# A gated linear attention and a squared-ReLU network on one core: scores as 64-by-64 tiles, a new order at the front, and another queue for the last store

## The chip, the core and the metric

The kernel runs on one core of a Trainium2 chip. A core has five engines with instruction streams of their own: TensorE (PE in the profile; PEld is its weight load), VectorE (DVE), ScalarE (ACT), GpSimd (POOL) and SyncE (SP), which here only issues transfers. ScalarE and GpSimd issue transfers too. The metric is the device time of one execution in microseconds, as the median of several runs.

## The reference

For each of 4 sequences and 8 heads of width 48 the attention runs a complex state over 768 tokens, and the tokens it gives go through a feed-forward network with 2048 hidden values:

```python
mag = np.sqrt(a_re * a_re + a_im * a_im)
scale = np.minimum(mag, 0.999) / (mag + 1e-06)
ar, ai = a_re * scale, a_im * scale
for t in range(S):                        # per batch and head, D = 48
    S_re, S_im = ar * S_re - ai * S_im + k[t] v[t]^T, ar * S_im + ai * S_re
    y[t] = q[t] @ S_re
x = y as (batch * S, heads * 48)          # 3072 x 384
h = np.maximum(x @ w_in, 0.0)             # w_in 384 x 2048
out = (h * h) @ w_out                     # w_out 2048 x 384
```

The two weight matrices arrive as 64-bit floats, that is as pairs of 32-bit words; the kernel turns them into 32-bit floats on the chip ("decoding").

## The kernel before

**Work and tiles.** A chunk is 128 tokens of one sequence. Two sequences go side by side, so that 12 groups of two chunks are worked one after the other: in the plan below the chunk of the first sequence of group g is called a*g*, the other b*g*. Eight heads lie on the 128 partitions in pairs: head rows 0 to 47 and 64 to 111, and the last pair's heads in the gaps of 16 rows between them ("gap" transfers fill these from the input; "last heads" copies bring their products into place again, L901).

For a chunk, `make_operands` turns raw gates, queries and keys into scaled operands on VectorE and ScalarE: squares (L773), sum of squares (L787), two steps of an inverse root (L792 to L805), gates (L825 to L829), running products in blocks and over blocks, and four products `qk` (L895). After the fourth product SyncE copies the last heads (`last<-qk`, L901). Then `chunk` does the attention: `scores` first applies the state carried from the chunk before (y, L936; not for the first chunk of a sequence) and then builds the scores of the chunk (a_ps, L944); keys are turned (tp, L951), the scores masked on VectorE (L963), summed over values (y, L970), the tokens copied to x (L981), and the new state added up (add, L994). The feed-forward network follows: `first_product` (h_ps, L1047 for single chunks in the first two groups, L1063 for both chunks later), squared ReLU on ScalarE, and the second product (o_ps, L1083 and L1153).

**The order of the work** is written out by hand: `FRONT` (L1187) is a string of some 1,400 tokens, and `follow` calls one function for each in that order, which fixes the order on every engine's stream and on every queue. The letters that matter here: `M` small preparations (`turn_mask`: M0 warms a function table on ScalarE, M1 builds the mask, M2 to M8 are memsets on VectorE), `l` loads of features (`load_parts`, L505), `v` loads of values, `f` and `j` fetch a weight block's words on SyncE and GpSimd, `D` and `A` are the two VectorE steps of decoding a block (L632 the shift, L635 the low part, with `U` and `S` on ScalarE ahead of the latter), `p`, `q` and `o` steps of `make_operands` for an a chunk, a b chunk or both, `a` and `b` steps of `chunk`, `g` gap copies of x, `F` and `H` first product and squared ReLU, `T`, `Z`, `R` parts of the second product and its sums, `s` stores, `K` a last test of ranges.

**Scores.** For each of four pairs, two components and two head rows one matmul has a stationary operand of 48 rows and 128 columns and 128 moving columns: 16 matmuls, which the profile shows as 32 rows. The two head rows lie in different halves of the array's rows. y L936 does its work with stationary operands of 48 by 64.

**Loads of features** (L519, L529): for each chunk and half of the rows one large transfer, followed on its queue by small gap transfers; SyncE takes one half, ScalarE or GpSimd the other.

**Stores** (L1117): all on SyncE, but for the last chunk, whose left half is stored by ScalarE and right half by SyncE. Behind them each engine loads a count (L1362) and jumps over a second way of computing (L1363), which is not taken; a closing barrier ends the program.

Of the kernel before, what the change touches and what calls it, by code (L numbers as in the profile page):

```python
# [32 lines left out]
ROWS = 64  # L33
LEVELS = 7
HALF = 64
RE, IM = 0, 1
# [390 lines left out]
def quotient_path(ctx, tc, feat, vtok, w_in, w_out, w1, w2, out, n_seq, count):  # L427
# [77 lines left out]
    def load_parts(gi, part=None, second=False, only=None):  # L505


        part = None if part == 2 else part
        parts = [slice(A_RE, Q), slice(Q, V), slice(A_RE, V)][2 if part is None else part]
        queues = [nc.sync, nc.scalar if part == 0 else other if gi < TWO_QUEUES else nc.sync]  # L510
        if part != 0 and gi < TWO_QUEUES:
            queues[not second] = None
        for b, n in enumerate(groups[gi]):
            if only not in (None, b):
                continue
            for hh, queue in enumerate(queues):
                if queue is None:
                    continue
                queue.dma_start(  # L519
                    out=raw[rows(hh), parts, b].rearrange("d x g t -> d x (g t)"),  # L520
                    in_=feat[n, hh, :, parts, 0:NG].rearrange("d x g t -> d x (g t)"))

                if part == 0 and b:
                    queue = nc.gpsimd
                gap = raw[pads(hh), parts, b]
                rest = feat[n, hh].rearrange("(r g) x p t -> r x g p t", g=NG)[:, parts, :, NG]
                for i in range(min(gap.shape[1:3])):
                    at = (slice(None), i) if gap.shape[1] < NG else (slice(None), slice(None), i)
                    queue.dma_start(out=gap[at], in_=rest[at])  # L529

    def in_turn(rows_, n):

# [382 lines left out]
    def chunk(gi, b):  # L915
# [7 lines left out]
        def scores():  # L923
# [17 lines left out]
            for p_ in range(NP):  # L941
                for c in (RE, IM):
                    for hh in range(HH):
                        nc.tensor.matmul(ps[:, hh, p_], lhsT=operand(2 + c, p_, rows(hh)),  # L944
                                         rhs=operand(c, p_, rows(hh)), start=(c == RE),
                                         stop=(c == IM))

        def keys_turned(c):
            tp = tiles["tp"] = pm.tile([C, NG, P], F32, tag="m", name="tp")
# [161 lines left out]
    def store(i, b):  # L1111

        queue, cols = nc.sync, slice(0, DM)
        if i == NGR - 1 and b:
            queue, cols = (nc.scalar, slice(0, MH)) if b == 1 else (nc.sync, slice(MH, DM))
        b = min(b, 1)
        queue.dma_start(out=in_turn(out, groups[i][b])[:, :, cols], in_=out_of[i, b][:, cols])  # L1117

# [38 lines left out]
    def outputs(i, r):  # L1157
# [27 lines left out]


    FRONT = (  # L1187
        "M8 l0.0.0 M2 M3 M7 l0.0.1 M1 M0 p0.0 p0.1 p0.3 p0.4 p0.5 p0.7 p0.2 q0.0 q0.3 p0.8 p0.9 "
        "p0.10 q0.4 q0.5 p0.11 q0.7 l0.1.0 f0 f1 l0.1.1 v0.0 f2 i0.1.0 j0 j2 q0.1 p0.12 p0.22 "
        "q0.8 q0.2 U0 q0.9 p0.6 q0.10 S0 p0.15 p0.23 p0.24 D0 p0.25 M4 p0.13 M5 p0.16 q0.11 "  # L1190
        "p0.26 i0.1.1 j1 D1 p0.27 A0 p0.17 p0.14 j3 i1.2.0 U1 S1 U2 q0.12 p0.18 q0.6 S2 q0.22 "
        "A1 f4 l1.2.0 f3 j4 p0.19 q0.15 p0.20 q0.23 p0.28 q0.24 p0.29 q0.25 p0.30 q0.16 D2 "
        "q0.26 q0.13 q0.27 A2 q0.17 p0.21 f6 a0.1 a0.2 U3 q0.14 a0.0 a0.3 U4 S3 q0.18 p1.6 a0.4 "
        "S4 a0.5 a0.6 l1.2.1 a0.7 D3 q0.19 M6 a0.8 q0.28 q0.20 p1.0 p1.3 q0.29 D4 q0.30 i1.2.1 "
        "q1.0 p1.4 p1.5 j6 j5 p1.1 p1.2 j7 g0.0 f5 v0.1 q0.21 f7 p1.7 p1.10 p1.9 p1.8 A3 A4 "
        "F0.1.0 U5 a0.9 U6 S5 D5 b0.1 b0.0 p1.11 b0.2 p1.12 S6 H0.1.0 A5 U7 b0.3 b0.4 S7 p1.15 "
        "D6 p1.23 b0.5 F0.0.0 b0.6 b0.7 f8 p1.24 A6 p1.25 q1.3 p1.16 D7 p1.26 A7 p1.27 D8 p1.17 "
        "F0.2.0 H0.0.0 q1.4 H0.2.0 U8 p1.22 S8 F0.3.0 b0.8 H0.3.0 p1.18 p1.13 p1.14 A8 g0.1 f11 "
        "F0.2.1 f9 f10 v1 p1.19 p1.20 p1.28 D9 p1.29 p1.30 q1.5 U9 q1.1 H0.2.1 q1.7 D11 b0.9 "
        "D10 F0.3.1 T0.0.0 H0.3.1 S9 A9 U10 q1.8 S10 q1.9 q1.2 q1.10 F0.0.1 F0.1.1 p1.21 f12 "  # L1200
        "f13 A10 q1.6 U11 q1.11 q1.12 S11 U12 a1.0 a1.1 T0.1.0 a1.5 a1.6 a1.7 S12 D13 D12 A11 "
        "q1.15 q1.23 A12 T0.2.0 T0.3.0 a1.2 U13 H0.0.1 q1.22 H0.1.1 a1.3 T0.4.0 q1.24 q1.25 "
        "q1.16 q1.26 q1.13 q1.27 q1.17 f14 g1.0 f15 S13 q1.14 l2 F1.2.0 H1.2.0 A13 F1.0.0 "
        "F1.3.0 q1.18 a1.4 U14 H1.3.0 U15 S14 i2 S15 q1.19 q1.28 q1.20 q1.29 D14 q1.30 A14 D15 "
        "A15 q1.21 a1.8 T0.5.0 F1.1.0 T0.6.0 T0.7.0 o2.0 o2.1 o2.3 o2.4 E0.0 o2.5 o2.2 b1.0 "
        "o2.7 a1.9 b1.5 T0.0.1 T0.1.1 b1.3 T0.2.1 b1.6 T0.3.1 T0.4.1 T0.5.1 T0.6.1 T0.7.1 o2.8 "
        "o2.9 o2.10 H1.1.0 b1.7 s0.0 v2 g1.1 w0 o2.11 o2.12 o2.15 o2.22 o2.13 o2.6 H1.0.0 "
        "F1.0.1 F1.1.1 E0.1 o2.14 b1.4 H1.1.1 l3 T1.0.0 b1.1 H1.0.1 F1.3.1 T1.1.0 T1.2.0 T1.3.0 "
        "T1.4.0 T1.5.0 T1.6.0 T1.7.0 o2.23 o2.24 o2.25 o2.16 o2.26 o2.27 o2.17 o2.18 o2.19 "
        "o2.28 o2.20 o2.29 o2.30 F1.2.1 o3.0 o3.6 o3.3 o3.4 o3.5 b1.2 o3.7 E1.0 b1.8 b1.9 o2.21 "  # L1210
        "a2.0 a2.5 t0 a2.1 T1.0.1 T1.1.1 o3.2 o3.1 o3.8 a2.2 o3.10 o3.9 a2.3 a2.6 a2.4 a2.7 "
        "H1.2.1 o3.11 o3.12 W0 a2.8 b2.0 a2.9 o3.22 H1.3.1 b2.5 T1.2.1 T1.3.1 b2.6 T1.4.1 "
        "T1.5.1 T1.6.1 b2.7 T1.7.1 g2 F2.0 o3.13 o3.15 o3.23 o3.24 o3.25 o3.16 o3.26 o3.27 "
        "o3.17 o3.14 H2.0 o3.18 o3.19 o3.28 o3.20 o3.29 o3.30 F2.2 H2.2 F2.4 H2.4 l4 s1.0 b2.1 "
        "F2.1 o4.0 H2.1 o3.21 s0.1 v3 F2.6 H2.6 b2.2 o4.3 F2.5 F2.7 o4.2 o4.4 o4.5 H2.7 X2.0 t1 "
        "X2.2 Y2.2 t3 H2.5 Y2.0 o4.7 b2.3 a3.0 b2.4 E1.1 s1.1 X2.1 Y2.1 a3.5 Z2.1 b2.8 a3.6 "
        "o4.1 o4.8 o4.9 Q2.0 b2.9 a3.3 a3.7 o4.10 a3.4 o4.11 F2.3 H2.3 Z2.0 a3.1 b3.0 X2.3 R2.0 "
        "o4.6 o4.22 Z2.3 a3.2 b3.5 b3.6 b3.7 o4.12 Y2.3 o4.13 Q2.3 Q2.1 o4.15 o4.23 Q2.2 o4.24 "
        "a3.8 a3.9 Z2.2 R2.3 Z2.5 o4.14 R2.2 R2.5 R2.1 o4.25 o4.16 o4.26 o4.27 o4.17 g3 F3.2 "
        "H3.2 F3.0 b3.3 b3.4 Z2.4 H3.0 o4.18 o4.19 o4.20 o4.28 o4.29 o4.30 F3.4 H3.4 F3.6 R2.4 "  # L1220
        "H3.6 X3.2 X3.0 F3.5 F3.1 b3.1 H3.5 F3.7 w1 l5 o5.0 t2 Z2.6 o5.3 o5.1 o5.4 H3.1 b3.2 "
        "o5.5 R2.6 o5.7 X3.1 o4.21 s2.1 s2.0 W1 w2 v4 F3.3 H3.3 H3.7 o5.2 Z3.0 b3.8 a4.0 X3.3 "
        "b3.9 Y3.1 Y3.2 a4.1 a4.5 Y3.0 Z3.1 R3.0 o5.6 o5.9 a4.2 o5.8 a4.3 Q3.0 o5.10 R3.1 o5.11 "
        "Q3.2 Y3.3 a4.6 a4.4 a4.7 a4.8 b4.0 a4.9 b4.1 Z3.2 Z3.3 o5.12 o5.22 b4.2 W2 b4.3 b4.4 "
        "R3.2 b4.5 b4.6 R3.3 b4.7 b4.8 o5.15 o5.23 o5.24 o5.25 Q3.1 Q3.3 o5.16 o5.13 Z3.4 Z3.5 "
        "w3 g4 o5.14 R3.4 o5.26 R3.5 F4.5 H4.5 l6 o5.27 o5.17 o5.18 o5.19 o5.20 v5 o5.28 F4.1 "
        "H4.1 X4.1 o5.29 F4.0 F4.4 o5.30 H4.0 o6.0 W3 H4.4 o6.3 b4.9 F4.3 Z3.6 H4.3 o6.4 F4.2 "
        "H4.2 o6.5 R3.6 o6.2 o6.1 F4.6 o6.7 H4.6 o5.21 s3.0 a5.0 F4.7 s3.1 o6.9 o6.8 a5.5 a5.6 "
        "o6.10 a5.7 H4.7 Z4.0 b5.0 Z4.1 Y4.1 o6.11 X4.3 Y4.3 X4.0 o6.6 w7 o6.22 o6.12 W7 R4.0 "
        "b5.5 X4.2 o6.15 Y4.0 Q4.0 R4.1 b5.6 Y4.2 Q4.1 Z4.2 R4.2 b5.7 o6.23 o6.24 Q4.2 o6.25 "  # L1230
        "o6.16 Z4.3 o6.13 Q4.3 o6.26 Z4.4 R4.3 Z4.5 R4.5 o6.27 o6.17 R4.4 o6.14 g5 F5.2 H5.2 "
        "o6.18 F5.4 F5.0 H5.4 o6.19 o6.28 o6.20 o6.29 o6.30 F5.3 Z4.6 l7 w6 H5.0 W6 a6.3 F5.1 "
        "o7.1 R4.6 H5.3 H5.1 F5.6 o7.0 H5.6 a6.4 X5.0 o7.3 o7.4 o7.5 F5.7 s4.0 o6.21 w8 v6 F5.5 "
        "a6.0 v7 a6.1 Z5.0 H5.5 W8 H5.7 o7.2 a6.2 w4 s4.1 X5.2 a6.5 Y5.0 Y5.2 o7.7 a6.6 a6.8 W4 "
        "o7.9 o7.8 R5.0 o7.10 b6.0 w9 W9 a6.7 Z5.1 X5.1 a6.9 b6.5 Q5.0 X5.3 Q5.2 Y5.1 Y5.3 R5.1 "
        "o7.11 Z5.2 o7.12 b6.3 R5.2 b6.4 Z5.3 b6.1 Z5.4 Q5.3 o7.15 o7.23 o7.24 o7.25 Q5.1 o7.16 "
        "w5 R5.3 b6.2 o7.22 W5 R5.4 b6.6 b6.8 Z5.5 Z5.6 b6.7 w10 g6 F6.1 o7.13 o7.26 o7.27 R5.5 "
        "o7.14 o7.6 o7.17 o7.18 o7.19 o7.28 o7.20 o7.29 o7.30 H6.1 F6.6 F6.5 l8 R5.6 H6.6 W10 "
        "v8 o7.21 s5.0 w14 s5.1 H6.5 F6.2 H6.2 F6.0 o8.0 o8.2 H6.0 b6.9 X6.2 Y6.2 o8.3 F6.4 "
        "a7.1 F6.3 o8.4 o8.5 H6.3 o8.6 H6.4 a7.0 a7.5 X6.1 a7.2 F6.7 H6.7 o8.1 X6.0 o8.7 o8.8 "  # L1240
        "o8.10 Z6.0 a7.3 R6.0 o8.9 Z6.1 Y6.0 X6.3 Y6.3 Y6.1 Q6.0 Q6.2 Z6.2 a7.4 W14 a7.6 a7.7 "
        "R6.2 a7.8 o8.11 a7.9 b7.0 Q6.3 R6.1 b7.5 w13 W13 o8.12 b7.1 b7.2 o8.22 Z6.3 R6.3 o8.13 "
        "o8.15 Q6.1 o8.23 o8.24 b7.6 b7.3 Z6.4 b7.7 b7.4 g7 o8.14 Z6.5 o8.25 R6.5 o8.16 o8.26 "
        "o8.27 o8.17 R6.4 b7.8 F7.5 F7.0 H7.5 o8.18 H7.0 F7.1 w15 W15 H7.1 l9 F7.4 o8.19 o8.28 "
        "o8.20 o9.0 H7.4 F7.2 F7.6 H7.2 o8.29 X7.1 o8.30 o9.3 o9.4 o9.5 o9.7 Y7.1 o9.1 Z6.6 "
# [150 lines left out]
```

## Time and profile before

| | us |
|---|---|
| median of 3 runs | 664.95 (664.70 to 665.57) |
| the profiled execution | 666.06 |
| its span, first to last instruction | 664.1 |
| PE busy | 616.7 |
| DVE busy | 493.2 |
| ACT busy | 434.9 |
| mean granted clock of PE | 0.996 |

The span is cut into 40 slices of 16.6 us; a digit is the busy share of a slice in tenths. The chain of waits is followed back from the last instruction, at each step to what released it. In a table of groups "xcount" counts rows, and one matmul of 32-bit floats makes two rows. Some rows of this profile that are used later (busy us and mean ns of one row; then idle time of the engine ahead of them):

| group | rows | busy, mean | 
|---|---|---|
| L944 a_ps<-qk, 48x128 by 128 | 576 | 39.9, 287 |
| L944 a_ps<-last, 48x128 by 128 | 192 | 15.8, 280 |
| L936 y, 48x64 by 128 | 640 | 22.8 + 12.2, about 275 |
| L994 add, 128x64 by 48 | 640 | 23.0, 226 |
| L1047 h_ps, 128x128 by 128 | 384 | 46.4, 281 |

A mean here is the length of a row in the pipeline, and rows overlap; the pace is read from the chain.

### The profile page before, as it was taken

Reading aid. Unit: us, or ns where it says so; the run is one execution under the profiler, and the core shown is the slowest. Engines: PE = TensorE matmul, PEld = TensorE weight load, DVE = VectorE, ACT = ScalarE, POOL = GpSimd, SP = SyncE. Lnnn points to the kernel's source line nnn. Section 1 sums busy time; section 2 is a strip of 40 time slices with the busy share of each in tenths; the row PEclk is TensorE's granted clock in tenths of the full one; section 3 lists DMA queues with packets and bytes.
Section 4 is the critical chain, followed back from the end, with each engine's and each line's share of the span. In section 5 each row is a group of like instructions: output and inputs, shape, how many; then the busy total and the mean of one; then the engine's idle time right before and its main releaser. Section 6 shows DMA issues by size and latency. Waiting matters only on the chain.

```text
span 664.1 us, 13108 instructions
## 1 busy us (share of the span) xinstructions
PE 616.7 (93%) x5147; PEld 552.0 (83%) x5147; DVE 493.2 (74%) x981; ACT 434.9 (65%) x847; POOL 31.9 (5%) x74
## 2 busy tenths in 40 slices
PE   0068999999999999999999999999999999999996
PEld 0057987776889899989899899899999899989996
DVE  4999888979997969858849948968849858753030
ACT  7668989757584585494586785686685675644331
POOL 5230110000000000000000000000000000000000
PEclk9998999999999999999999999999999999999999
DMA  8986863540634331730842813542631620232101
GB/s 198 167 160 148 257 192 68 92 56 21 95 72 82 55 87 32 119 73 10 142 142 55 142 51 79 96 109 72 113 95 32 108 65 21 67 84 79 47 26 30
DMA packets 41744, 60.41 MB, mean 91 GB/s; under 512 B 5832, under 2 KB 29896, under 8 KB 41672
## 3 DMA queue, kind: packets, MB, share of 16 engines
q1 hardware_dynamic: 39360, 55.39, 38.7%
q0 software_dynamic: 1824, 3.64, 3.0%
q8 instruction: 42, 0.69, 0.5%
q10 hardware_dynamic: 488, 0.44, 0.2%
q14 instruction: 30, 0.25, 0.1%
HBM read 48.76 MB, written 4.72 MB: 81 GB/s over the span
## 4 chain that ended last, share of the span: by engine, by line
PE 91%; DVE 5%; DMA 2%; ACT 1%; issue 1%; ACTq 0%; POOL 0%; DVEq 0%; SPq 0%
PE h_ps L1063 31%; PE o_ps L1153 28%; PE a_ps L944 7%; PE o_ps L1083 6%; PE h_ps L1047 6%; PE y L970 4%; PE y L936 3%; PE add L994 3%; PE tp L951 2%; DVE ab L494 1%; DMA last<-qk 1%; DVE pr L494 1%; DMA raw<-in_feat_dram 1%; DVE qk L494 0%; DMA words<-in_moe_w_in_dram 0%
## 5 line engine op out<-in xcount | busy, mean ns | idle before, releaser
L1063 PE MATMUL h_ps<-x,w 128*128 128x256 f32 x960 | 212.4, 379 | 0.0
L1063 PEld LDWEIGHTS h_ps<-x,w 128*128 128x128 f32 x960 | 180.9, 190 | 24.1 <-ACT h L1070 0.2
L1153 PE MATMUL o_ps<-w,h 128*128 128x192 f32 x640 | 110.5, 328 | 0.0
L1153 PEld LDWEIGHTS o_ps<-w,h 128*128 128x128 f32 x640 | 103.8, 190 | 1.9 <-issue 0.5
L1070 ACT ACTIVATE h<-h_ps 128x512 f32<-128x512 f32 x80 | 47.5, 594 | 69.5 <-PE h_ps L1063 67.3
L494 DVE TENSOR_TENSOR pr<-ab 128x384 f32<-128x384 f32 (+3 forms) x196 | 70.1, 375 | 4.3 <-ACT ab L833 0.9
L1153 PE MATMUL o_ps<-w_sum,mix 128*128 128x192 f32 x320 | 55.3, 328 | 0.0
L494 DVE TENSOR_TENSOR a<-a_ps,mask 128x1024 f32<-128x1024 f32 x24 | 29.3, 1222 | 33.6 <-PE a_ps L944 33.5
L494 DVE TENSOR_TENSOR ab<-pr 128x48 f32<-128x48 f32 (+3 forms) x210 | 49.9, 260 | 5.3
L1153 PEld LDWEIGHTS o_ps<-w_sum,mix 128*128 128x128 f32 x320 | 51.7, 190 | 0.7 <-issue 0.2
L1071 ACT ACTIVATE h<-h 128x512 f32<-128x512 f32 x80 | 50.5, 631 | 2.5
L951 PE MATMUL tp<-ident,qk 128*128 128x128 f32 x120 | 21.5, 291 | 30.3 <-DVE qk L494 30.0
L1047 PEld LDWEIGHTS h_ps<-x,w 128*128 128x128 f32 x384 | 45.6, 197 | 4.0 <-DVE w L494 1.3
L1047 PE MATMUL h_ps<-x,w 128*128 128x128 f32 x384 | 46.4, 281 | 2.2 <-DMA x<-x 1.1
L494 DVE TENSOR_TENSOR qk<-ab,qk 128x768 f32<-128x768 f32 (+1 forms) x56 | 46.1, 842 | 1.0
L1083 PE MATMUL o_ps<-w,h 128*128 128x384 f32 x128 | 44.3, 492 | 0.0
L951 PEld LDWEIGHTS tp<-ident,qk 128*128 128x128 f32 x120 | 14.8, 146 | 35.3 <-issue 31.7
L981 ACT COPY x<-y 64x256 f32<-64x256 f32 (+1 forms) x72 | 26.5, 368 | 24.9 <-PE y L970 23.4
L944 PE MATMUL a_ps<-qk 48*128 48x128 f32 x576 | 39.9, 287 | 0.0
L494 DVE TENSOR_TENSOR mix<-h 128x256 f32<-128x256 f32 x40 | 16.8, 420 | 30.9 <-ACT h L1071 30.9
L758 ACT ACTIVATE qk<-raw 128x768 f32<-128x768 f32 (+1 forms) x28 | 37.4, 1341 | 3.6 <-DVE raw L494 3.6
L494 DVE TENSOR_TENSOR room<-ab,carry 128x1344 f32<-128x1344 f32 (+1 forms) x28 | 36.8, 1354 | 3.6 <-ACT carry L874 2.8
(106 smaller groups left out, 923.4 us busy)
## 6 DMA issues: line engine op xcount, KB each, us to landing
raw<-in_feat_dram SPq DMA_DIRECT2D x40, 288.0 KB
words<-in_moe_w_out_dram SPq DMA_DIRECT2D x8, 768.0 KB
again<-in_moe_w_in_dram SPq DMA_DIRECT2D x16, 384.0 KB
again<-in_moe_w_out_dram SPq DMA_DIRECT2D x16, 384.0 KB
last<-qk SPq DMA_DIRECT2D x48, 97.5 KB
words<-in_moe_w_in_dram SPq DMA_DIRECT2D x8, 576.0 KB
vt<-in_vtok_dram SPq DMA_DIRECT2D x24, 192.0 KB
out_dram<-o SPq DMA_DIRECT2D x23, 192.0 KB
```

What stands on the lines that cost most here:

```text
L494: nc.vector.tensor_tensor(out=out, in0=in0, in1=in1, op=op)
L758: nc.scalar.activation(out=out.rearrange("p c j n -> p c n j"), func=AF.Copy, in_=in_.rearrange("p c (n j) -> p c n j", j=L), **kwargs)
L944: nc.tensor.matmul(ps[:, hh, p_], lhsT=operand(2 + c, p_, rows(hh)), rhs=operand(c, p_, rows(hh)), start=(c == RE), stop=(c == IM))
L951: nc.tensor.transpose(tp[:, g], qk_of[gi % 2][:, b, g, 2 + c, 0:C], ident)
L970: nc.tensor.matmul(tiles["y"][p_ % 2][crossed(hh, p_), p_ // 2], lhsT=v[:, columns(hh, at)], rhs=tiles["am"][:, hh, p_], start=(first and ...
L981: nc.scalar.copy(out=x_of[gi][to, odd::2, b * C:(b + 1) * C], in_=tiles["y"][odd][of, 0:NP // 2])
L1047: nc.tensor.matmul(ps[:, j], lhsT=w1_blocks[:, k, g, at:at + P], rhs=x_of[i][:, g, b * C:(b + 1) * C], start=(g == 0), stop=(g == NG - 1))
L1063: nc.tensor.matmul(ps[:, j], lhsT=w1_blocks[:, k, g, at:at + P], rhs=x_of[i][:, g], start=(g == 0), stop=(g == NG - 1))
L1070: nc.scalar.activation(out=h, in_=h_ps[i, f], func=AF.Relu, scale=of_w1)
L1071: nc.scalar.activation(out=h, in_=h, func=AF.Square)
L1083: nc.tensor.matmul(o_of[i, b], lhsT=tokens_of(i, f, b)[:, j], rhs=w2[:, k], start=(k == 0), stop=(k == NFB - 1))
L1153: nc.tensor.matmul(to, lhsT=x(k)[:, j], rhs=factor(z)[:, 2 * k + j], start=(z in (0, 1, 3) and k == j == 0), stop=(k == KH // 2 - 1 and j ...
```

## The change

In `load_parts` the gap transfers of the first part (gates) of a chunk a0 go ahead of the large one on their queue; for the other parts the order stays:

```diff
-                queue.dma_start(
-                    out=raw[rows(hh), parts, b].rearrange("d x g t -> d x (g t)"),
-                    in_=feat[n, hh, :, parts, 0:NG].rearrange("d x g t -> d x (g t)"))
-
-                if part == 0 and b:
-                    queue = nc.gpsimd
                 gap = raw[pads(hh), parts, b]
                 rest = feat[n, hh].rearrange("(r g) x p t -> r x g p t", g=NG)[:, parts, :, NG]
-                for i in range(min(gap.shape[1:3])):
-                    at = (slice(None), i) if gap.shape[1] < NG else (slice(None), slice(None), i)
-                    queue.dma_start(out=gap[at], in_=rest[at])
+                pieces = [(slice(None), i) if gap.shape[1] < NG else (slice(None), slice(None), i)
+                          for i in range(min(gap.shape[1:3]))]
+                moves = [(gap[at], rest[at]) for at in pieces]
+                whole = (raw[rows(hh), parts, b].rearrange("d x g t -> d x (g t)"),
+                         feat[n, hh, :, parts, 0:NG].rearrange("d x g t -> d x (g t)"))
+                if part == 0 and b:
+                    queue.dma_start(out=whole[0], in_=whole[1])
+                    queue = nc.gpsimd
+                else:
+                    moves.insert(len(moves) if part == 0 else 0, whole)
+                for to, of in moves:
+                    queue.dma_start(out=to, in_=of)
```

In `scores` each matmul becomes two, one for each half of the stationary columns and of the output's partitions:

```diff
-                        nc.tensor.matmul(ps[:, hh, p_], lhsT=operand(2 + c, p_, rows(hh)),
-                                         rhs=operand(c, p_, rows(hh)), start=(c == RE),
-                                         stop=(c == IM))
+                        for s in (slice(0, ROWS), slice(ROWS, C)):
+                            nc.tensor.matmul(ps[s, hh, p_],
+                                             lhsT=operand(2 + c, p_, rows(hh))[:, s],
+                                             rhs=operand(c, p_, rows(hh)), start=(c == RE),
+                                             stop=(c == IM), skip_group_check=True)
```

Both halves of the last chunk's store are issued by SyncE:

```diff
-            queue, cols = (nc.scalar, slice(0, MH)) if b == 1 else (nc.sync, slice(MH, DM))
+            cols = slice(0, MH) if b == 1 else slice(MH, DM)
```

The plan has the same tokens in another order up to F4.1, the first product of group 4; from there on it is unchanged. Its beginning, and the part around the last heads of chunk b0 (q0.21):

```diff
-        "M8 l0.0.0 M2 M3 M7 l0.0.1 M1 M0 p0.0 p0.1 p0.3 p0.4 p0.5 p0.7 p0.2 q0.0 q0.3 p0.8 p0.9 "
...
-        "q1.0 p1.4 p1.5 j6 j5 p1.1 p1.2 j7 g0.0 f5 v0.1 q0.21 f7 p1.7 p1.10 p1.9 p1.8 A3 A4 "
...
+        "l0.0.0 l0.0.1 M1 M0 p0.0 p0.1 p0.3 p0.4 p0.5 p0.7 M2 M3 p0.2 q0.0 q0.3 M8 M6 M7 p0.9 "
...
+        "D5 q0.29 q1.3 q0.30 U5 p1.4 p1.5 g0.0 f6 F0.1.0 S5 q0.21 p1.7 A4 a0.9 b0.1 p1.2 p1.10 "
+        "p1.8 p1.9 p1.1 U6 b0.2 p1.11 A5 b0.0 f7 v0.1 p1.12 H0.1.0 S6 U7 p1.22 p1.15 b0.5 p1.23 "
```

Numbers of lines shift by 3 to 5 in the changed kernel.

## The prediction

> **What bounds the kernel now.** I read the page's slices first, then the chain of waits for the whole span, then that chain in windows, then groups by shape. The slices say which stretch belongs to whom:
>
> ```profile
> PE   0068999999999999999999999999999999999996
> DVE  4999888979997969858849948968849858753030
> PE 91%; DVE 5%; DMA 2%; ACT 1%; issue 1%; ACTq 0%; POOL 0%; DVEq 0%; SPq 0%
> ```
>
> The reader is to see two regimes. In the first three and a half slices (to about 58 us) TensorE (PE) is mostly idle and VectorE (DVE) full; from there to the last slice PE is full, and the chain gives it 91% of the span. A change counts for what it takes off PE's work after 58 us, for what it does to the moment at which PE becomes continuous, or for the last 6 us. The table of stretches has PE busy 20.00 of 20 us in 60 to 80 us, 200.00 of 200 in 300 to 500: after 58 us there is no idle time to win, only work.
>
> The window of the chain at 185 us shows what a scores block costs in place:
>
> ```profile
> 185.58 1.03 PE y L936 x32
> 186.61 1.99 PE a_ps L944 x32
> 188.60 2.80 PE o_ps L1153 x16
> 191.39 1.07 PE add L994 x32
> 196.42 2.60 PE o_ps L1153 x16
> 206.19 0.92 PE add L994 x32
> ```
>
> (start, length, engine, tile, line, rows; a matmul is two rows in this trace.) The same 16 rows of o_ps take 2.60 us behind other 128-by-128 work and 2.80 behind a scores block; add takes 1.07 behind o_ps and 0.92 behind y L970 of its own shape. So each change of tile shape on PE costs 0.15 to 0.20 us.
>
> The last view is the chain at the front, where PE waits:
>
> ```profile
> 49.92 0.08 SPq L901
> 50.05 6.70 DMA last<-qk
> 56.79 0.71 PE a_ps L944 x6
> 58.25 3.81 PE h_ps L1047 x22
> ```
>
> The copy of the last heads of chunk b0 leaves SyncE (SP) when VectorE has made the fourth product, takes 6.70 us, and the last scores of that chunk wait for it; PE is continuous from there.
>
> **The change part by part.**
>
> *Scores as 64 by 64.* Each of 24 blocks goes from 32 rows (48x128 stationary, 128 moving columns) to 64 rows (48x64). Streaming: 12 rows of h_ps L1047 with 128 columns take 1.34 us, 0.111 a row, over the whole array. 16 pairs of 64x128 tiles are 16 x 0.111 = 1.78; the block takes 1.99, so 0.21 is the price of entering its shape. y L936 already has 64x64 tiles: 32 rows as 8 fours are 0.89 of its 1.03, entry 0.14. The new block is 16 fours, again 1.78. What goes is the entry, where y L936 stands right ahead in the same shape: 20 blocks (all but the first chunk of each of the four sequences). 20 x 0.19 (between 0.14 and 0.21) = 3.8; the four others swap an entry of 0.21 for 0.14, 0.3. Sum -4.1 us, all on PE's path.
>
> Here a rule speaks against the change. The Trainium skill, "TensorEngine Tiling (Array Packing)", section Instruction Overhead, gives each matmul some 60 cycles that don't shrink, and warns against taking a tiling factor from what is already small. At the 2.4 GHz of "Trainium Kernel Development and Optimization", NeuronCore Architecture, that is an estimated 25 ns; put on top of the 32 added rows of each block it is 768 x 25 ns = 19 us lost, not 4 won. The rows say otherwise: y L936 runs 32 rows of just this shape in 1.03 us with its entry, add L994 32 rows of 48 columns in 0.92 (28.7 ns a row). As a floor of 28.7 against 27.8 from streaming, it costs 64 x 0.9 ns x 24 = 1.4 us. I take y's pace, the same shape, and keep -2.7 as the end of the range. The same page, Key Properties, says that a change of tiling mode drains PE: that is the entry seen above.
>
> *The plan's order on PE.* Counting shape changes along both plans, with the scores already fused, gives 101 before and 98 after (y L970 and add stand together more often): 3 x 0.17 = -0.5. From F4.1 (about 320 us) the plans are equal.
>
> *The front on ScalarE and the transfers.* "Table warmed first": in the changed program ScalarE's order is still DMA issues, table load, the two mask copies, table load, warm-up, squares. In the profile the loads are 1.28 us each, at 3.27 and 5.93, and the first squares start at 7.33. Nothing is removed: 0. The gap transfers ahead of the large one concern only chunk a0 of the first part; SP and ScalarE issue as many as before (0.6 to 0.8 us each). The large transfers of chunk a0 leave 1.4 to 1.7 us later, at about 2.6; transfers issued at that time landed in 3 to 3.7 us, so at 6.3 at most, under cover of the table load to 7.2. Without that cover it would be 0.6 to 1 us. I take 0 (0 to +0.5).
>
> *The front on VectorE.* The memsets M8, M2, M3, M7 lay in its idle time before 8.19 (5.05 us waiting for the first squares). They now stand behind the first inverse: begun 0.70, qk 0.15, states 0.78, 1.63 us. VectorE still waits there for ScalarE (1.24, 0.24 and 0.82 us before 9.98, 11.38 and 12.76); the first wait is ahead of them, the two others take up 1.0. So +0.65 at the second inverse. Up to the fourth product of chunk b0 the new order also has one more decode low part (w<-w,part, 0.87), one more shift (L632, 0.50) and one sum of squares of group 1 (L787, 0.48). Walking both orders row by row they are level at 42.4 us (one decode went later), and behind it stand two decodes, a shift and a sum of squares more: 2 x 0.87 + 0.50 + 0.48 - 0.1 (memset kt, gone ahead) = +2.6. The fourth product ends at 52.0 in place of 49.35, and SP's copy, queued behind it, leaves then.
>
> What that costs depends on the copy's own time. Before, a weight fetch (47.44) and the value load vt (47.96) went out just ahead of it, the next fetch just behind at 50.74: 6.70 us. The same copy for chunk a0 at 35.46, with nothing near, was done when GpSimd took it at 39.05: 3.6 us. Afterwards vt is moved behind it, past the next fetch, and the fetch ahead leaves about 4 us earlier than it. So landing is 55.6 at 3.6, 58.7 at 6.7; I take 56.0, near the free one: -0.7. The moved vt, behind the fetch on the queue, should land by 59; its reader y L970 of chunk b0 also needs the mask product, which VectorE reaches at about 60.0 (58.54 to 59.67 before), behind 24 rows of h_ps. The later decodes of blocks 4 to 7 end at 57 to 65 us, before PE's need. I take no new stall in 58 to 170 us, with +1 for the range.
>
> One more term: at 58.25 these 24 rows took 4.03 us where 2.68 is usual (granted clock 0.65 in 58 to 62.2). PE waits as long as before; I leave that 1.35 as it is, and a gain of it for the range.
>
> *The last store.* ScalarE issues it at 658.50 in 1.20 us, loads the count (0.69) and jumps; its first instruction behind the jump is at 663.17. SP's issues of stores take 0.60 to 0.71, so the data land some 0.5 earlier. But SP is now the late one: its branch comes at about 659.2 in place of 656.63, and SP needed 3.9 us from there to its next instruction (ScalarE 2.6, GpSimd 2.8, VectorE 3.5), then a row of some 20 semaphore waits at 0.065, 1.3, which it did under cover of ScalarE. 659.2 + 2.6 to 3.9 + 1.3 + 0.9 for the closing barrier = 664.0 to 665.3 against 664.1. Middle value +0.4 (-0.1 to +1.2).
>
> **Sum** against the profiled execution (span 664.1, its time 666.06): -4.1 - 0.5 + 0 - 0.7 + 0.4 = -4.9, 661.2. It is 1.1 over the median of the runs; on 664.95 the same sum gives 660.0.
>
> **The rivals.**
> 1. *The front takes some back.* For: VectorE is full there (9.86 of 10 us in 50 to 60), and 2.6 us are put before the copy. Against: the queue is freer. With 6.7 again (+1.9) and the tail's +1.2: -4.6 + 3.1 = -1.5, 663.4. Chance 0.14.
> 2. *The front gives more.* The copy at 3.6 (-1.1) and no lowered clock (-1.35), tail -0.1: -4.6 - 2.5 - 0.1 = -7.2, 657.7. Chance 0.13.
> 3. *Slower: the column halves don't overlap.* Two halves of one row group read the same moving rows; if they run one after the other, a row costs 55 ns, a block 64 x 0.0555 = 3.55 + 0.14, +1.7 x 24 = +41, 706 us. It decides from 31 ns a row (1.99 / 64). Against it: y L936's fours at 27.8. Chance 0.06.
> 4. *The change doesn't do what it says.* For the table this is so already. If the entry stays too, because each block waits for its first weights whatever its shape, -4.1 becomes 0 and the rest cancels: 664.5. Against: add's 0.92 behind its own shape. Chance 0.03.
>
> **How the numbers follow.** The sum above, 660.0, has chance 0.64; with its terms' ends (-2.7 to -4.5 for scores, -0.5 to +1.5 for the front, -0.1 to +1.2 for the tail), not all at one end, 658 to 662.5. The range reaches to rivals 1 and 2: 656.9 to 663.6. A measurement of this kernel tells 0.2%, 1.3 us, from no change. Cases 1 (in the main) and 2 and the likeliest are faster: 0.91; same 0.03; slower 0.06.
>
> **What would show it.** Right: a block of 64 rows of a_ps in 1.78 to 1.85 us behind y L936, with h_ps or o_ps behind it still 0.2 longer; squares again near 7.3; the last<-qk copy of chunk b0 issued near 52 and landed near 56; PE full from about 57; SP the last engine at the end. Wrong: rows of a_ps at over 31 ns; a copy landing at 58 or later; PE idle between 60 and 170 us for a weight or mask; squares waiting for the feature load.

## The result and the profile after

| | before | after |
|---|---|---|
| median of 6 runs each, us | 664.92 (664.63 to 665.57) | 661.35 (659.45 to 661.95) |
| the profiled execution | 666.06 | 661.44 |
| its span | 664.1 | 659.1 |
| time outside the span | 1.96 | 2.34 |
| PE busy | 616.7 | 611.2 |

The medians differ by 3.57 us, 0.54%. The ratio of the runs, which is not the quotient of the medians, is 0.9937 (95% interval 0.9924 to 0.9951); it stands for 4.2 us, between 3.3 and 5.1. Four of the six runs after lie between 661.2 and 662.0 and two near 659.5. The point forecast was 660.0, that is 4.95 us. By the medians 1.35 of them did not come, but 4.95 lies just inside the interval.

First the slices and the shares of the chain of waits in the profile after:

```profile
PE   0059999999999999999999999999999999999995
DVE  4999997998999948968759858879859858743030
PE 77%; DVE 10%; ACT 6%; DMA 5%; issue 1%; SPq 0%; DVEq 0%; ACTq 0%
```

PE is full from the fourth slice on, from the fifth before. But the chain gives PE 77% of the span, not 91%: followed back from the end it now leaves PE in several places, for VectorE, ScalarE and transfers. That is not lost time: behind 58.5 us PE stands idle for 0.33 us in all (0.06 at 152.1, 0.12 at 378.5, 0.15 at 553.8; in the profile of before no gap is over 0.04). Where another engine's work ends last, by however little, the chain goes on along that engine, so the 77% tells where slack has run out.

The chain at the same group of chunks as the window shown of before (start, length, engine, tile, line, rows):

```profile
185.37 1.03 PE y L939 x32
186.41 1.75 PE a_ps L948 x64
188.15 2.79 PE h_ps L1068 x12
```

The scores block has 64 rows in place of 32 and takes 1.75 us, 27.3 ns a row, in place of 1.99. A row over the whole array takes 0.111 us, four times that: four tiles run side by side. What follows in another shape still pays: 12 rows of h_ps take 2.79 us, and 2.59 behind their own shape (at 193.83 in the profile of before).

The chain at the front of the profile after:

```profile
46.49 3.73 DMA x<-x
50.22 0.24 issue
50.46 5.26 PE h_ps L1052 x24
55.72 0.33 PE tp L956 x3
56.05 1.91 PE a_ps L948 x64
57.96 2.88 PE h_ps L1052 x24
60.84 1.02 PE y L975 x16
```

The copy of the last heads is gone from it. SyncE issued it from 51.58, GpSimd could read it at 56.0, and PE, which came to the rows that need it at 57.34, did not wait. Instead the first 24 rows of the network take 5.26 us, twice their usual 2.7, and carry the chain to 55.72.

### The profile page after: what moved, and what is told of

It reads as the page before. It is cut to its first block, busy times and chain, and to the rows that moved or that the text cites. A ratio compares the mean times of both kernels' runs of the same rounds, so it can differ in the third digit from the quotient of the medians.

```text
span 659.1 us, 14644 instructions
## 1 busy us (share of the span) xinstructions
PE 611.2 (93%) x5915; PEld 549.0 (83%) x5915; DVE 492.1 (75%) x981; ACT 434.2 (66%) x847; POOL 33.2 (5%) x74
## 3 DMA queue, kind: packets, MB, share of 16 engines
q1 hardware_dynamic: 39496, 55.49, 39.2%
## 4 chain that ended last, share of the span: by engine, by line
PE 77%; DVE 10%; ACT 6%; DMA 5%; issue 1%; SPq 0%; DVEq 0%; ACTq 0%
PE h_ps L1068 29%; PE o_ps L1158 27%; PE a_ps L948 5%; PE h_ps L1052 4%; PE y L975 3%; DMA raw<-in_feat_dram 3%; PE y L939 3%; DVE ab L494 2%; PE add L999 2%; DVE pr L494 2%; PE tp L956 2%; PE o_ps L1088 1%; DMA words<-in_moe_w_out_dram 1%; ACT room L761 1%; ACT ab L761 1%; DVE room L494 1%
## 5 line engine op out<-in xcount | busy, mean ns | idle before, releaser
L1075 ACT ACTIVATE h<-h_ps 128x512 f32<-128x512 f32 x80 | 47.6, 595 | 57.8 <-PE h_ps L1068 56.7
L761 ACT ACTIVATE qk<-raw 128x768 f32<-128x768 f32 (+1 forms) x28 | 36.9, 1343 | 5.2 <-DVE raw L494 5.2
L761 ACT ACTIVATE room<-z 128x768 f32<-128x768 f32 (+1 forms) x28 | 36.8, 1373 | 5.1 <-DVE z L808 5.1
L761 ACT ACTIVATE ab<-raw 128x768 f32<-128x768 f32 (+1 forms) x28 | 37.8, 1375 | 0.5 <-DVE qk L494 0.3
```

Source lines behind the costliest of these rows:

```text
L761: nc.scalar.activation(out=out.rearrange("p c j n -> p c n j"), func=AF.Copy, in_=in_.rearrange("p c (n j) -> p c n j", j=L), **kwargs)
L1075: nc.scalar.activation(out=h, in_=h_ps[i, f], func=AF.Relu, scale=of_w1)
```

## The experiments

All times are medians; each ratio is against runs of the kernel before on the same chip (664.92, 665.13 and 665.31 us in the three sets of four) and can differ from the quotient of the medians by some 0.6 us.

**The scores alone.** The kernel before with this edit:

```diff
-                        nc.tensor.matmul(ps[:, hh, p_], lhsT=operand(2 + c, p_, rows(hh)),
+                        for s in (slice(0, ROWS), slice(ROWS, C)):
+                            nc.tensor.matmul(ps[s, hh, p_], lhsT=operand(2 + c, p_, rows(hh))[:, s],
```

> The kernel before with the split of the scores alone (old plan, old loads, old store). Theory E (the split saves the entry): the chain of the changed kernel shows y and its scores in 2.79 us together where they took 3.02 before (20 such pairs), and a block without y in 1.91 where it took 1.99 (4 blocks); 20 x 0.23 + 4 x 0.08 = 4.9 us off PE, of which new waits on the other engines may take back up to 1. So 660.0 to 661.0 us, ratio 0.9926 to 0.9940. Rival P (the new order of the plan carries the gain, the split is nearly free of effect): 664 to 665 us. A block of 64 rows behind y should again be at 1.75 us.

Measured: 661.47 us, ratio 0.9951 (0.9937 to 0.9965), so 3.5 us. The size is under the expected 3.9 to 4.9, the sign and the bearer are theory E's; rival P falls.

**The store alone.** The kernel before with `cols = slice(0, MH) if b == 1 else slice(MH, DM)` on SyncE for both halves.

> The kernel before with both halves of the last store issued by SyncE, nothing else. Theory E: the stretch from the last copy of o to the end grew from 5.96 to 6.65 us in the changed kernel, and nothing else there was changed; so +0.7 us, 665.3 to 665.9, with SyncE's first instruction behind its jump as the late one. Rival: SyncE's issue is shorter than ScalarE's (0.60 against 1.20 us), the branch doesn't matter, and it is -0.5 us, 664.4.

Measured: 665.17, ratio 1.0007 (0.9998 to 1.0015). The rival's gain of 0.5 lies outside the interval. The loss, 0.25 in the medians where 0.7 was expected, is not clear of none. From the start of ScalarE's last copy to the end it took 6.22 us, 5.99 in the kernel before; SyncE's first instruction behind its branch came 2.97 us after it.

**The changed kernel with ScalarE's store.** The same edit turned round.

```diff
-            cols = slice(0, MH) if b == 1 else slice(MH, DM)
+            queue, cols = (nc.scalar, slice(0, MH)) if b == 1 else (nc.sync, slice(MH, DM))
```

> The changed kernel with the left half of the last store given back to ScalarE. Theory E: -0.7 us against the changed kernel, 660.3 to 660.9 us, with the last stretch back at 6.0 us. Rival: SyncE's store was the gain, and this is slower than the changed kernel by 0.5, 661.9 us.

Measured: 660.80, ratio 0.9937 (0.9923 to 0.9950), 0.55 under the changed kernel. Run once more in the last set:

> The changed kernel with ScalarE's store once more, as the base of the two runs with early memsets on the same chip: 660.8 (660.1 to 661.2), 2.28 us outside the span.

Measured: 660.67, ratio 0.9930 (0.9917 to 0.9944), 2.27 us outside the span. The medians of all three have the sign of theory E, 0.25 to 0.7 us lost by SyncE's store. But no interval separates them: the ratio of the first of these two runs is that of the changed kernel itself. In the profiles the stretch from PE's last row to the end is 5.92 to 6.45 us in eight with ScalarE's store (mean 6.16) and 6.25 to 6.73 in six with SyncE's (mean 6.43): a loss of some 0.3, with ranges that overlap.

**The changed kernel with whole scores.** The diff of the first experiment turned round, in the changed kernel.

> The changed kernel with the scores whole again (48x128 stationary): new plan, new loads and new store alone. Theory E: front and shape changes -1.6 us (PE was 3.7 us ahead at the point from where the plans are equal, of which 8 x 0.23 + 2 x 0.08 = 2.0 belong to the scores), store +0.7: -0.9, so 664.0 us (663.4 to 664.8). Rival P (the plan carries the gain): 661 to 662 us.

Measured: 665.52, ratio 1.0009 (1.0001 to 1.0017). Both fall. Without the split the new plan, loads and store together are slightly slower than the kernel before, where theory E expected 0.9 us of gain. Against the store alone (665.17) plan and loads are worth +0.35; against the scores alone, the run with ScalarE's store puts them at -0.67. Together they are about nothing.

**The loads as before,** in the changed kernel.

> The changed kernel with the loads as before (large transfer first for chunk a0's gates too). The squares start at 7.36 us behind the table load in the changed kernel, 7.33 before, so theory E: no change, 661.35 within 0.4. Rival: the gap transfers' order moves the feature loads behind and costs 0.5, then this is 660.8.

Measured: 661.61, ratio 0.9953 (0.9940 to 0.9965). No gain from the old order, as theory E expected. The rival's 0.5 isn't seen, but the six runs spread from 659.24 to 663.34, so it is only made unlikely.

**A shape broken, and kept.** Two edits at one place, between y and the scores of each of 20 blocks:

```diff
+            if not first:
+                nc.tensor.matmul(ps[:, 0, 0], lhsT=ident, rhs=ident, start=True, stop=True)
```

```diff
+            if not first:
+                for hh in range(HH):
+                    for s in (slice(0, ROWS), slice(ROWS, C)):
+                        nc.tensor.matmul(ps[s, hh, 0], lhsT=operand(2, 0, rows(hh))[:, s],
+                                         rhs=operand(0, 0, rows(hh)), start=True, stop=True,
+                                         skip_group_check=True)
```

> The changed kernel with one 128x128 matmul (two rows, results overwritten) put between y and the scores of each of 20 blocks: the streaming is 0.22 us, and the block's shape is now entered anew. Theory E (the gain is the saved change of shape): 0.22 + 0.20 (out of y's shape) + 0.14 (into the scores') = 0.56 a block, 11 us, 672.5. Rival N (only the number of matmuls counts): 0.22 a block, 4.4 us, 665.8. Best read against the next run, which adds the same streaming in the scores' own shape: theory E 5.6 to 8 us more than that, rival N nothing.

> The changed kernel with four extra 48x64 matmuls (eight rows, results overwritten) between y and the scores of each of 20 blocks, the control for the run with one 128x128 matmul there: 8 x 27.3 ns = 0.22 us a block and no change of shape, so 4.4 us, 665.8 (665.2 to 666.5) by both theories. If the small matmuls had a price of their own above streaming, it would be more: at 55 ns a row 8.8 us.

Measured: broken 671.98, ratio 1.0107 (1.0092 to 1.0122); kept 664.48, ratio 0.9987 (0.9976 to 0.9999). The difference is 7.5 us, 0.375 a block. The chain of the broken run, where L945 is the one big matmul, and then of the kept run, where L947 is the four small ones:

```profile
186.57 1.03 PE y L939 x32
187.60 0.42 PE a_ps L945 x2
188.02 1.91 PE a_ps L950 x64
```

```profile
186.40 1.03 PE y L939 x32
187.44 0.22 PE a_ps L947 x8
187.66 1.75 PE a_ps L954 x64
```

The big matmul streams for 0.22 us and takes 0.42: 0.20 to leave the shape. The same 64 rows behind it take 1.91, behind four of their own 1.75: 0.16 to enter it. Eight rows more in the same shape cost 0.22, nothing above streaming. The sum of 0.36 a block agrees with the 0.375 of the run times. Theory E is shown, and N falls. One thing was missed: the kept run was expected at 665.2 to 666.5 and lies below, 3.1 us above the changed kernel where 20 x 0.22 is 4.4; why is open.

**The front filled.** With ScalarE's store:

```diff
+        if (i, two, b) == (0, 1, 0):
+            for _ in range(15):
+                nc.tensor.matmul(ps[:, 0], lhsT=ident, rhs=ident, start=True, stop=True)
```

> The changed kernel with ScalarE's store (660.80 us), and PE's idle stretch of 3.67 us ahead of the first 24 rows of the network (F0.1.0) filled with 15 matmuls of identity by identity into the product's own buffer, whose results are overwritten; at half pace 15 x 0.222 = 3.3 us. Theory C (the front's gain is eaten by TensorE's clock: the 24 rows take 4.8 to 5.4 us because PE stood idle): the 24 rows come down towards 2.7 us, PE then waits for the last heads of chunk b0 until about 56.0 where it now reaches them at 57.4, so -0.5 to -1.4 us, 659.4 to 660.3. Rival D (the pace of these rows comes from elsewhere): 24 rows again at about 5 us, no gain, 660.5 to 661.5.

Measured: 660.59, ratio 0.9932 (0.9920 to 0.9944): 0.2 under its base at most. PE's timeline there (the last bracket is the idle time ahead and who ended it):

```profile
46.77 4.60 PE L1051 MATMUL h_ps<-ident 128*128 128x128 f32 x30
51.21 2.84 PE L1055 MATMUL h_ps<-x,w 128*128 128x128 f32 x24
54.55 0.52 PE L956 MATMUL tp<-ident,qk 128*128 128x128 f32 x3 [0.50 <-DVE pr L494]
...
56.95 2.94 PE L1055 MATMUL h_ps<-x,w 128*128 128x128 f32 x24
60.46 1.09 PE L975 MATMUL y<-a,vt 128*64 128x128 f32 x16 [0.57 <-DMA vt<-in_vtok_dram]
```

Theory C is right on the pace: the 24 rows take 2.84. It is wrong on the worth. The 3.3 us expected for the filling are its time at full pace (15 x 0.222); it took 4.60, because its first rows ran slowly. So it held the 24 rows up by 0.65 us (to 51.21, where the base starts them at 50.56), and what was won above that turned into waits, for VectorE at 54.55 and for the value load vt at 60.46. y L975 of chunk b0 starts at 60.46; in its base it was 60.56.

**The memsets.** In the plan of the changed kernel with ScalarE's store, and the converse in the kernel before:

```diff
-        "l0.0.0 l0.0.1 M1 M0 p0.0 p0.1 p0.3 p0.4 p0.5 p0.7 M2 M3 p0.2 q0.0 q0.3 M8 M6 M7 p0.9 "
+        "M8 l0.0.0 M2 M3 M7 l0.0.1 M1 M0 p0.0 p0.1 p0.3 p0.4 p0.5 p0.7 p0.2 q0.0 q0.3 M6 p0.9 "
```

> The changed kernel with ScalarE's store (660.80 us) and the four memset steps M8, M2, M3, M7 back ahead of the first inverse, in VectorE's idle time (M6 stays behind). Two theories for the 0.35 us that each kernel with the new plan spends outside its span (2.24 to 2.35 us there against 1.87 to 2.09 with the old plan). Theory M (the late memsets, the only part of the new plan within the first 5 us): outside the span again 1.9 to 2.0, and VectorE's second inverse at about 15.3 in place of 15.71; -0.35 to -0.8 us, 660.0 to 660.5. Rival O (something else of the plan): 2.28 outside, VectorE's 0.43 hidden or not, 660.4 to 661.0.

> The kernel before with the memsets alone put where the new plan has them, all else as before. Theory M: outside the span 2.28 us in place of 1.93, the second inverse some 0.4 later; +0.35 to +0.8 us, 665.3 to 665.8. Rival O: outside 1.93 and at most +0.4, 664.9 to 665.3.

Measured: 660.75, ratio 0.9937 (0.9923 to 0.9951), 2.29 us outside the span; and 665.64, ratio 1.0011 (1.0004 to 1.0018), 1.93 outside. Theory M falls for the time outside the span in both, although the second time, 665.64, lies where it was forecast (665.3 to 665.8) and not in rival O's 664.9 to 665.3. For the memsets themselves the two runs give +0.1 and -0.3 us for having them early. VectorE's second inverse is 0.4 and 0.3 us later with late memsets; an effect of that size on the time isn't in both.

**One ReLU earlier.** On top of the early memsets:

```diff
-F6.0 o8.0 o8.2 H6.0
+F6.0 o8.0 H6.0 o8.2
```

> The run with the memsets first, and one step more: at about 376 us ScalarE makes the squared ReLU of F6.0 (H6.0) ahead of the squares of the next group (o8.2), because there PE waited 0.12 us and lost some 0.3 more around it for the buffer that this ReLU frees. If the wait is what the stall costs: -0.3 to -0.5 us against the run without this step where the stall occurs; if the chain behind it on VectorE takes its place: 0.

Measured: 660.24, ratio 0.9922 (0.9909 to 0.9936), the fastest median here, 0.5 under the run without the step; the intervals overlap, so it is a hint. What the step does in the traces stands below.

## Why the prediction was right or wrong

The gain comes from the scores, as predicted, and the total lies in the range. One step of the sum, the front, did not hold for the median, and one loss, outside the span, was not in it.

**Scores: right, and somewhat better than summed.** A pair of y and scores took 3.02 us before and 2.78 after, 0.24 and not 0.19; 20 x 0.24 + 4 x 0.08 = 5.1 on PE where -4.1 was predicted. From y L975 of chunk b0 to PE's last row, the scores-only profile has 591.22 us and the store-only one, with the same plan, 596.16: 4.94 (4.67 and 4.83 against the two other profiles with the old plan and whole scores). This stretch holds 22 of the 24 blocks. The term is mis-sized in two small ways: the whole entry of 0.21 went, where 0.19 was taken, and the rows run at 27.3 ns, where 27.8 was taken, 0.03 a block. The medians show less of it than PE's work, 3.5 to 4.2; the profile of the scores-only run is its fastest execution (660.48 against 661.47), and where its other executions lost 1 us no trace shows.

The 19 us that the prediction estimated from the Trainium skill ("TensorEngine Tiling (Array Packing)", Instruction Overhead) did not come: eight rows more of 48x64 took 0.22 us, all of it streaming. The prediction had put the page's some 60 cycles on top of each row. The page's next line reads as a floor instead, a moving size of 1 taking as long as one of 60, and the rows agree with that: add L994 with 48 columns takes 28.7 ns a row, where 48/128 of y L970's 55.6 would be 20.9, and 128 columns lie above such a floor. The drain that the page's Key Properties name is there: leaving a shape took 0.20 and entering one 0.16, and the saved entry is 0.21 of the 0.24 us a pair. Rival 3 needed over 31 ns a row and falls by the same rows. Rival 4, an entry that is paid whatever the shape, falls by the 1.75 us behind y and 1.91 behind another shape.

**Shape changes in the plan: right in sign, -0.2 to -0.46 for -0.5.** With whole scores, the same stretch is 596.08 in the new plan and 596.16 in the old; the new one has three rows of tp more behind that point (0.38 to the next block): 596.08 - 0.38 - 596.16 = -0.46. Against the 595.89 of the profile of before it is -0.19: profiles of one plan differ by that much. The prediction put the point from which the plans are equal at about 320 us; the traces have it at 267.5 before and 263.8 after, and nothing rested on it.

**"No new stall in 58 to 170 us": the place held but for 0.06 us at 152; stalls came later.** They come with PE being earlier. The one at 553.8, where a second product waits for ScalarE's copy of the sums (o, L1031), is 0.15 to 0.18 us in eight of the ten profiles with the split; the four with whole scores, and the two in which added rows hold PE back, don't have it. The larger one is at 376 us, here in the chain after:

```profile
375.21 1.49 ACT room L776
376.70 1.48 ACT ab L761
378.18 0.43 ACT h L1075
378.61 0.04 issue
378.65 2.86 PE h_ps L1068 x12
```

h_ps needs the buffer that the ReLU L1075 frees, and this stands on ScalarE behind the squares L761 of the next group. On PE the three rows of tp ahead start at 378.04, h_ps at 378.65 where 0.33 behind is usual, and the y behind it at 381.44: 3.40 us. ScalarE's timeline in the run with the ReLU moved ahead:

```profile
376.01 0.58 ACT L1075 ACTIVATE h<-h_ps 128x512 f32<-128x512 f32 x1
376.62 0.63 ACT L1076 ACTIVATE h<-h 128x512 f32<-128x512 f32 x1
377.16 1.54 ACT L761 ACTIVATE ab<-raw 128x768 f32<-128x768 f32 x1
```

The ReLU now goes ahead of L761. There tp starts at 377.56, h_ps at 377.88 and y at 380.57: 3.01 us, so the stall is 0.4 us that the sum did not have. It shows in three of the profiles with the split (0.10 to 0.23 us of pure idleness) and in none without it. But it isn't in every execution: the profile of the run with early memsets, the base of the moved ReLU, has the old order and 3.02 us there as well. So the trace shows what the stall costs, and not that the moved step removed it.

**The front: this step failed.** The prediction took 0.7 us off because the copy of chunk b0 would land at 56.0 and not 56.7 and PE be continuous that much sooner. The copy did as told: issued from 51.58 (52.0 was said), its reader on GpSimd released at 56.0. But PE stood long for it only in the profiled execution of before (0.66 and 0.27 us). In the other profiles with the old plan PE came to this block of scores 1.1 to 1.7 us later (at 54.90 to 55.44, here at 53.76), and less of the wait was left. The lines of before and of the kernel before with late memsets, where the copy took 6.89 us:

```profile
56.03 0.48 PE L944 MATMUL a_ps<-last 48*128 48x128 f32 x2 [0.66 <-DMA last<-qk]
56.79 0.71 PE L944 MATMUL a_ps<-last 48*128 48x128 f32 x6 [0.27 <-DMA last<-qk]
```

```profile
56.46 0.48 PE L944 MATMUL a_ps<-last 48*128 48x128 f32 x2
57.30 0.71 PE L944 MATMUL a_ps<-last 48*128 48x128 f32 x6 [0.36 <-DMA last<-qk]
```

In the scores-only run PE's weight loads waited 0.4 us for the copy, in the store-only run nothing on PE is put down to it. Two executions of the same front, the windows of before and of the store-only run (columns: PE busy, granted clock, DMA share, GB/s):

```profile
56.00:60.00 4.00, 3.70 (x21) 0.69 0.86 273
60.00:64.00 4.00, 4.00 (x38) 0.88 0.00 0
```

```profile
56.00:60.00 4.00, 4.00 (x49) 1.00 0.94 284
60.00:64.00 4.00, 4.00 (x43) 1.00 0.06 17
```

In the first the clock was high early (the first 24 rows of the network, in two halves from 48.77, ran at full pace), PE then stood waiting for the copy, and the clock dropped to half for 3.4 us from 57.6. In the second, PE ran these 24 rows slowly, from 49.66 in 5.46 us, reached the scores at 55.49 when most of the copy's time had gone by, and had no drop. (The column of the granted clock prints 1.00 where the trace has no record of it, and in the second the first record is at 55.07; ahead of it the pace of the rows tells.) Start of y L975 (L970 before) of chunk b0: 62.22 in the profile of before; 60.79, 61.09 and 61.10 in three others with the old plan; 59.43 to 61.14 in those with the new. The profile of before is 1.1 us over its median, which is about this drop (1.35). Against the three others the changed kernel's 60.77 is 0 to 0.3 us sooner, not 0.7. So the profiled difference, 4.62, holds 1.1 to 1.4 us of front that the medians don't. The prediction saw both numbers (a profile 1.1 above the median, 24 rows 1.35 too long), put them down separately, and carried the sum over to the median unchanged. Rival 2's lowered clock did go away, but likewise between the two profiles and not between the medians.

The memsets, +0.65 at the second inverse, measured 0.43 (15.28 to 15.71). The moved value load was to land by 59; with the front filled it landed at 60.3, 6.83 us from its issue, later than y could have started. PE waited 0.57 us for it there and 0.55 in the kept-shape run. With whole scores in the new plan y waited 0.66 us at 60.48, put down to VectorE. So in three profiles with the new plan PE, when it comes early, is stopped again at y, a wait that the prediction took as free.

**Outside the span: not in the sum.** Every kernel with the new plan spends 2.24 to 2.31 us outside its span (medians of the sets), every one with the old plan 1.93 to 1.97. That is 0.34 lost which no row of a trace shows. The split, the store, the loads and the memsets are each excluded as its sole cause by a run that has one without the other. It goes with the remaining order of the plan; why stays open.

**The last store: right in place, its size not settled.** +0.4 was said; the profiled stretch grew by 0.7 (5.99 to 6.69 from ScalarE's last copy to the end), the medians say 0.25 to 0.7, within their scatter. SyncE branched 1.02 us after that copy's start and took 3.4 to its next instruction, as the prediction had it late.

**The sum, for the medians.** Two ways lead through the runs from the kernel before to the changed one. Scores alone, then plan and loads, then SyncE's store: -3.45, -0.67, +0.55. Or store, plan and loads, scores: +0.25, +0.35, -4.17. Both end at -3.57 because they must; what they tell is how far each term is known. Of the 1.35 us that the medians lack, the front's 0.7 and the 0.34 outside the span make up the most; the rest lies within the scatter of the runs. That the total came so near has some luck in it: PE's gain on the scores was sized 1 us too small in the profile, and this made up for part of what the front did not give and the span did not hold.

Rival 1 had the nearer mechanism in one respect, that the front gives nothing clear, but not its cause: the copy did not come late.

## What to carry to other kernels

Count changes of tile shape in the instruction stream of a full TensorE, and make neighbours alike: it was worth 0.24 us a block here, even at twice the number of matmuls. Before a front is costed from one execution, ask whether its time stands on the median, and take a stall that is only in that execution out of the sum, on both sides. Where the bound engine gets 4 us earlier, look for those of its releasers that have less slack than that; both stalls that came were of a short ScalarE step that stood in line behind other work.

## What the runs showed of the hardware that was not expected

The granted clock of TensorE stepped in pieces of 3.41 us, or multiples of it, in all fourteen profiles. Four have a piece at half while PE works at the front: from 57.6 in before, and from 50.2, 50.2 and 50.5 in three with the split and the new plan (early memsets, old loads, broken shape). The last record at full clock starts between 52.8 and 61.0 us in thirteen of them, and at 48.9 in the one with the filled front. In the changed kernel four of the six runs lie at 661.25 to 661.95 (mean clock 0.997 to 0.998), and two at 659.45 and 659.69 (0.995). That the clock at the front parts them is likely and not shown, as these runs have no trace of their own; in the kernel with late memsets it was the slow runs that had the low mean (667.79 us at 0.995, 665.10 at 0.999). The profile of the early-memsets run is a fast one, 659.29 us where its median was 660.75:

```profile
48.00:52.00 4.00, 2.23 (x12) 0.78 0.79 202
52.00:56.00 4.00, 4.00 (x65) 0.80 1.01 217
```

Its first 24 rows took 4.54 us in place of 5.26, with a clock that was lowered inside them, and y of b0 started at 59.43. Only the filled front was made to act on the clock, and had these rows at full pace; for the others, which way an execution goes stays open.
